# A fused RWKV-7 state update and gated convolution: chunks of 64 tokens, every product on 64x64 tiles of TensorE, decays by scans both ways

## The chip, the cores and the metric

The kernel runs on one core of a Trainium2 chip. A core has TensorE (PE, with its weight loads PEld), VectorE (DVE), ScalarE (ACT), GpSimd (POOL) and SyncE (SP, which issues the DMAs). The metric is device time in microseconds from the first to the last instruction of one execution.

## The reference

A recurrence over 768 tokens for 4 x 8 = 32 independent heads of 40 channels, then a gated short convolution between two matrix products over 320 channels. All of it is float32.

```python
for t in range(S):                                     # S = 768; state is 40 x 40 for each of 32 (b, h)
    y[:, :, t] = np.einsum('bhd,bhde->bhe', rt, state)
    Sa = np.einsum('bhde,bhe->bhd', state, at)
    state = state * wt[:, :, None, :] - np.einsum('bhd,bhe->bhde', Sa, bt) + np.einsum('bhd,bhe->bhde', vt, kt)
...
gate = 1.0 / (1.0 + np.exp(-gate_pre))                 # gate_pre: causal convolution of 5 taps over x = y
out = (gate * (x @ w_val)) @ w_out                     # 320 x 320 matrices
```

## The kernel before

The tokens are cut into 24 chunks of C = 32. Inside a chunk the recurrence is turned into matrix products: a running product of the decays w (`lam`, the scan of line 344) scales a, and its inverse (logarithm and exponential on ACT, a Newton step on DVE, lines 357 to 366) scales k and b (`atil`, `ktil`, lines 371 and 377). The products of a with k and b (`amat`, line 385) give two strictly triangular 32x32 matrices for each of the 32 units (a unit is one batch and head). One is inverted by substitution on DVE: four chunks make one group whose triangles stand side by side, and 30 steps of two operations each (`step`, lines 430 and 433: a product into `tm`, a subtraction from `x`) do all of them at once, with 32x32 block transposes around them (lines 422 and 451).

The serial part runs chunk after chunk, in two halves of 16 units (`hf`): `stage_u0` (lines 492 and 493) multiplies with v and with the state, `stage_uu` (531 and 534) applies the inverted triangle, `stage_g` (560) forms the products with r, `stage_ys` (576 and 577) yields output and new state, and `stage_st` (608) transposes the state for the next chunk. Results go from PSUM to SBUF by copies on ACT and masked products on DVE. Two chunks of outputs are then moved by DMAs from units to channels (`xe` to `xt`), convolved (738, DVE), gated (748 to 753: three functions on ACT, one DVE operation and one more function on ACT), multiplied with `w_val` (85, 93), gated (769), multiplied with `w_out` (103) and stored.

In `stage_u0` each unit has two matrix products into one PSUM region: line 492 contracts over 64 rows (two units share the 128 partitions), line 493 over 128 rows, and the two alternate. `stage_uu` has products of 64 rows and 64 or 40 columns, in which four neighbouring ones use four different 64x64 quarters of the array.

`Plan` holds every operation with an engine, a length in ns and what it waits for, and makes one order for each of PE, ACT, DVE and POOL. Each engine executes its order strictly, so an operation that waits holds up all that stand behind it. Where the plan leaves PE idle, the last loop puts in matrix products on a constant tile (`dm`, line 808), whose results nobody reads; there are 364 rows of them in the trace.

The constants' loading, the conversion of the weights from 64-bit floats on DVE (lines 50 to 57), and a second path for inputs whose decays leave a range (not taken here) stand in both versions.

Of the kernel before, what the change touches and what calls it, by code (L numbers as in the profile page):

```python
# [17 lines left out]
C = 32  # L18
P16 = 16
ER = 104  # L20
DM = 320
NW = P16 * 33
NE = P16 * C
EWF = NW + 3 * NE
NWT = 1280 + DM + 15
WB = 323
UO = 184
X0 = [(0, 0, D, 0, 0), (1, 0, D, 0, 40), (2, 0, 8, 0, 120), (2, 8, 16, 1, 120), (3, 0, D, 2, 0), (2, 16, D, 2, 40)]
X1 = [(4, 0, D, 0, 80), (5, 0, D, 1, 0), (6, 0, D, 1, 40), (7, 0, D, 1, 80)]
NCST = 128 + 32 + 64 + 64 + 32 + 128  # L30
NQ, NL = 7, 8
WLO, WHI = 0.5, 2.0
NB = 1
LAT = 180
NIT = 4
FB = 3
TS = 11000
GAP = 200
TH = 5000
WIN = 3413  # L40
RHO = {"uu": 0.9, "v": 0.9, "w": 1.4, "u0": 1.3, "am": 1.4, "g": 1.4, "kbt": 1.5, "st": 1.5}
# [54 lines left out]
def out_mms(nc, ps, gv, wo, j, n):  # L96
    T = nc.tensor
    L = n * C
    if n == 2:
        for k in range(3):  # L100
            r = slice(j * 64, j * 64 + 64) if k == 2 else slice(0, 128)
            q = 8 if k == 2 else 4 * k + 2 * j
            T.matmul(out=ps, lhsT=gv[r, q * L:q * L + 128], rhs=wo[k][r], start=(k == 0), stop=(k == 2))  # L103
# [9 lines left out]
def moe_steps(nc, mo, pp, wts, wz, xe, xt, store):  # L113
    V, A = nc.vector, nc.scalar
    L, w = C, B * C
# [25 lines left out]
    out_mms(nc, ps[:, 0:DM], gv.rearrange("p b t -> p (b t)"), wo, 0, 1)  # L141
# [6 lines left out]
class Plan:  # L148
    """Operations with an engine, a length and what they wait for, put into an order engine by engine."""
# [4 lines left out]
    def op(self, name, eng, dur, deps, fn, lat=None):  # L154
        assert name not in self.ops, name
        self.ops[name] = [eng, dur, list(deps), fn, LAT if lat is None else lat]

    def order(self):
        ops = {n: [e, d, [x for x in dp if x in self.ops], f, l] for n, (e, d, dp, f, l) in self.ops.items()}
        succ = {n: [] for n in ops}  # L160
        left = {}
        for n, o in ops.items():
            left[n] = len(o[2])
            for x in o[2]:
                succ[x].append(n)
        topo, stack, cnt = [], [n for n in ops if not left[n]], dict(left)
# [10 lines left out]
        def lag(x, y):  # L177
            return ops[x][4] if ops[x][0] != ops[y][0] else (0 if ops[x][0] in ("PE", "SP") else 127)
# [5 lines left out]
        pred = {n: o[2] for n, o in ops.items()}  # L184

        def place(seq, before, gap):
            """Each operation of seq into the first gap of its engine after what it waits for."""
            free = {e: [[0.0, 1e12]] for e in {o[0] for o in ops.values()}}
            when = {}

            def find(e, t, d):
                f = free[e]
                i = bisect.bisect_right(f, [t, 1e13]) - 1
                i = max(i, 0)
                while True:
                    u = max(f[i][0], t)
                    if u + d <= f[i][1]:
                        return u
                    i += 1

            def take(e, t, d):
                f = free[e]
                i = bisect.bisect_right(f, [t, 1e13]) - 1
                lo, hi = f[i]
                f[i:i + 1] = [x for x in ([lo, t], [t + d, hi]) if x[1] - x[0] > 1]

            for n in seq:
# [750 lines left out]
```

## Time and profile before

| | before |
|---|---|
| times of three runs, us | 712.37, 716.68 (median), 718.1 |
| span of the profiled execution, us | 712.3 (the lowest of the times is 712.37) |
| mean granted TensorE clock | 0.805 of full speed |
| PE / DVE / ACT / POOL busy, us | 647.2 / 474.2 / 384.7 / 177.8 |

A busy time is the union of the engine's instructions in the trace. A float32 matrix product of the program is two MATMUL rows in the trace, a transpose on PE is one; neighbouring matrix products overlap, so the length of one row says little, and the time of a stage is read from the stretch that it fills. The granted clock has two levels here, 0.5 and 1.0 of full speed (1.2 and 2.4 GHz).

### The profile page before, as it was taken

To read this page: it belongs to the slowest core of one execution; us is meant where nothing else is said; L and a number is where in the kernel's file an instruction comes from. 1 tells how busy PE (TensorE), PEld (TensorE's weight loads), DVE (VectorE), ACT (ScalarE), POOL (GpSimd) and SP (SyncE) were. 2 spreads that over 40 slices of the span, in tenths; PEclk is the share of its full clock that TensorE was granted. 3 is DMA by queue.
4 is the path that set the end of the run, shared out by engine and by line. 5 is a ranking of instruction groups with operands and counts; after the bars stand their busy time and mean duration, and the time that the engine had idled before them with its cause. 6 is when DMAs were issued, how large, how long until landed. Compare 5 with 4: busy or idle time off the path is not lost.

```text
span 712.3 us, 19169 instructions
## 1 busy us (share of the span) xinstructions
PE 647.2 (91%) x7701; PEld 509.5 (72%) x7701; DVE 474.2 (67%) x1151; ACT 384.7 (54%) x1167; POOL 177.8 (25%) x146
## 2 busy tenths in 40 slices
PE   1687899998999989899999999999999999999983
PEld 0566787887777768677777687777778787777772
DVE  7958956358577775956766676879656646895140
ACT  3426564446457754664754547676644663556430
POOL 7674323022332250423222032122202011100000
PEclk9957766568788876867877878999968779999996
DMA  8642322142142334233241152171302121212010
GB/s 210 152 118 63 93 53 63 40 114 69 46 107 72 83 101 102 69 87 80 63 118 50 52 129 67 60 177 43 106 28 75 37 64 56 71 55 69 20 32 12
DMA packets 26400, 55.31 MB, mean 78 GB/s; under 512 B 6564, under 2 KB 17060, under 8 KB 23812
## 3 DMA queue, kind: packets, MB, share of 16 engines
q1 hardware_dynamic: 26308, 54.05, 29.2%
q8 instruction: 62, 1.02, 0.6%
q14 instruction: 30, 0.25, 0.1%
HBM read 45.90 MB, written 3.93 MB: 70 GB/s over the span
## 4 chain that ended last, share of the span: by engine, by line
PE 65%; DVE 12%; ACT 8%; DMA 7%; SPq 3%; issue 2%; POOL 1%; DVEq 0%; ACTq 0%; POOLq 0%
PE pc L493 15%; PE pc L492 14%; PE pm L103 5%; PE pm L85 4%; DMA out<-xt 4%; PE pc L576 4%; SPq L314 3%; PE pp L408 3%; PE pp L385 3%; PE sg L608 3%; PE sg L560 3%; PE pc L577 2%; PE pc L518 2%; DVE mm L569 2%; PE pc L517 2%
## 5 line engine op out<-in xcount | busy, mean ns | idle before, releaser
L493 PE MATMUL pc<-st,qa 128*64 128x64 f32 x768 | 142.8, 274 | 0.0
L492 PE MATMUL pc<-v,akb 64*64 64x64 f32 x768 | 139.8, 268 | 1.1 <-DVE xe L601 1.1
L499 ACT COPY us<-pc 64x160 f32<-64x160 f32 x96 | 27.5, 287 | 159.1 <-PE pc L493 158.4
L492 PEld LDWEIGHTS pc<-v,akb 64*64 64x64 f32 x768 | 82.5, 150 | 34.3 <-DVE xe L601 1.3
L493 PEld LDWEIGHTS pc<-st,qa 128*64 128x64 f32 x768 | 84.1, 155 | 31.2
L569 DVE TENSOR_TENSOR mm<-sg,cst 64x128 f32<-64x128 f32 x192 | 55.4, 289 | 50.4 <-PE sg L560 45.1
L738 DVE SCALAR_TENSOR_TENSOR ag<-xt,wts,ag 128x256 f32<-128x256 f32 (+2 forms) x156 | 65.7, 449 | 16.6 <-ACT ag L736 16.4
L576 PE MATMUL pc<-mm,lh 128*40 128x80 f32 x768 | 71.9, 248 | 1.8 <-DVE mm L569 1.6
L577 PE MATMUL pc<-mm,lh 128*40 128x80 f32 x768 | 70.6, 248 | 2.5 <-DVE mm L569 2.5
L371 POOL TENSOR_TENSOR qa<-ew,lam 40x512 f32<-40x512 f32 x24 | 45.1, 1879 | 105.5 <-PE pc L493 93.3
L417 ACT COPY lh<-pp 64x160 f32<-64x160 f32 x192 | 55.1, 287 | 30.0 <-PE pp L408 26.1
L377 POOL TENSOR_TENSOR kb<-ew,y 104x512 f32<-104x512 f32 x24 | 47.9, 1997 | 79.0 <-PE pp L408 47.1
L576 PEld LDWEIGHTS pc<-mm,lh 128*40 128x40 f32 x768 | 60.5, 126 | 7.2 <-DVE mm L569 2.4
L577 PEld LDWEIGHTS pc<-mm,lh 128*40 128x40 f32 x768 | 59.6, 125 | 6.5 <-DVE mm L569 6.1
L430 DVE TENSOR_TENSOR tm<-x 128x30 f32<-128x30 f32 (+9 forms) x180 | 63.2, 351 | 1.5
L471 POOL MEMSET mm<- 40x640 f32 x22 | 13.8, 627 | 200.6 <-PE pc L576 106.5
L433 DVE TENSOR_TENSOR x<-x,tm 128x30 f32<-128x30 f32 (+9 forms) x180 | 60.8, 338 | 1.7
L617 ACT COPY lh<-sg 40x160 f32<-40x160 f32 x184 | 52.8, 287 | 15.1 <-PE sg L608 12.9
L542 ACT COPY vu<-pc 40x128 f32<-40x128 f32 x192 | 49.8, 260 | 16.0 <-PE pc L534 13.4
L551 ACT COPY mm<-pc 32x160 f32<-32x160 f32 x192 | 54.4, 284 | 2.8
L456 POOL TENSOR_TENSOR akb<-akt,cst 128x512 f32<-128x512 f32 x24 | 35.9, 1494 | 69.7 <-PE pc L492 56.5
L385 PE MATMUL pp<-kb,qa 104*64 104x64 f32 x768 | 38.4, 267 | 16.3 <-POOL kb L377 14.5
(109 smaller groups left out, 1209.4 us busy)
## 6 DMA issues: line engine op xcount, KB each, us to landing
ew<-in_ew SPq DMA_DIRECT2D x24, 838.5 KB
vu<-in_vt SPq DMA_DIRECT2D x24, 416.0 KB
mm<-in_rp SPq DMA_DIRECT2D x48, 100.0 KB
v<-in_v SPq DMA_DIRECT2D x24, 160.0 KB
mm<-in_vn SPq DMA_DIRECT2D x48, 80.0 KB
out<-xt SPq DMA_DIRECT2D x24, 160.0 KB
xt<-xe SPq DMA_DIRECT2D x66, 42.5 KB
ag<-in_wts SPq DMA_DIRECT2D x3, 323.0 KB
```

What stands on the lines that cost most here:

```text
L385: T.matmul(out=st_["ap", c][b2 * 64:b2 * 64 + 64, u * 64:u * 64 + 64], lhsT=QA[c % NQ][0:ER, p], rhs=st_["kb", c][:, p], start=True, stop= ...
L417: A.copy(out=dst[:, i], in_=pv[i * 64:i * 64 + 64, :, par * 64:par * 64 + D])
L430: V.tensor_tensor(out=tv, in0=x[:, j:j + 1, j + 1:32].to_broadcast([128, j, n]), in1=x[:, 0:j, j:j + 1].to_broadcast([128, j, n]), op=ALU. ...
L433: V.tensor_tensor(out=x[:, 0:j, j + 1:32], in0=x[:, 0:j, j + 1:32], in1=tv, op=ALU.subtract)
L492: T.matmul(out=o, lhsT=akb[r, u], rhs=v4[r, u * D:u * D + 64], start=True, stop=False)
L493: T.matmul(out=o, lhsT=qa[:, p], rhs=st[:, p - 8 * hf], start=False, stop=True)
L551: A.copy(out=dst, in_=src)
L569: V.tensor_tensor(out=dst, in0=ps[r, :, par], in1=maskG[r].unsqueeze(1).to_broadcast([64, 4, C]), op=ALU.mult)
L576: T.matmul(out=ps[0:40, hl, b * 80:b * 80 + 80], lhsT=lh[:, 0, p * D:p * D + D], rhs=mm[:, 0, :, p], start=True, stop=True)
L577: T.matmul(out=ps[64:104, hl, b * 80:b * 80 + 80], lhsT=lh[:, 1, p * D:p * D + D], rhs=mm[:, 1, :, p], start=True, stop=True)
L617: A.copy(out=dst[:, i], in_=pv[i * 64:i * 64 + 40, :, r0:r0 + D])
L738: V.scalar_tensor_tensor(out=acc[:, q], in0=xt[:, q, i:i + L], scalar=cw[:, k, i:i + 1], in1=acc[:, q], op0=ALU.mult, op1=ALU.add)
```

## The change

The kernel's fast path is written anew. The chunk is 64 tokens, so there are 12; the serial part is passed through 12 times.

**Decays.** One scan gives the running product over 64 tokens (`LAM`, line 306); a second scan, over the same data from the back and started for each unit with the reciprocal of the product's last value (line 548, 16 numbers), gives its inverse (line 308). The logarithm, the exponential and the Newton step are gone.

**Products on 64x64 tiles.** Each unit stands alone on 64 partitions and 64 columns (40 channels padded to 64, or 64 tokens). Every stage of the serial part issues products of four quarters of the array in turn. Where two products add into one PSUM region (`pairs`), the first of each pair stands in a first half of the stage and the second in the second half, with a drain of PE between.

**Triangles.** The inverse of a 64x64 triangle is made of two inverted 32x32 triangles, by the same 30 steps of two DVE operations, and a corner that two small stages on PE form from them (`fmat`, `zmat`, 32x32 tiles). A group is two chunks, which fill the same 128 x 1024 numbers as four chunks of 32 did; there are 7 groups (one chunk, five times two, one chunk). POOL clears the upper half before the steps (`tri`) and spreads the result (`expand`).

**The rest.** The masks are applied on POOL (`akm`, `gm`), to tiles that ACT has copied from PSUM, and the scaling of a, k and b is on POOL from the third chunk on. The gate is one Sigmoid. The matrix products on the constant tile are gone. The plan has other lengths and no repeated passes, and now orders SP as well; PSUM tiles (P, Q, R, M, two banks each) have one holder at a time.

```diff
-C = 32
+C, GC = 64, 32
...
-    A.activation(out=gv, in_=acc, func=AF.Abs)
-    A.activation(out=gv, in_=gv, func=AF.Exp, scale=-1.0)
-    A.activation(out=gv, in_=gv, func=AF.Ln, bias=1.0)
-    V.scalar_tensor_tensor(out=acc, in0=acc, scalar=0.0, in1=gv, op0=ALU.min, op1=ALU.subtract)
-    A.activation(out=acc, in_=acc, func=AF.Exp)
+    A.activation(out=acc, in_=acc, func=AF.Sigmoid)
...
+    def scan(c, back):
+        w = W[c % 2]
+        if not back:
+            V.memset(ind2[:, 0:NW - 1:C + 1], 1.0)
+            V.tensor_tensor_scan(out=LAM[c % NA].rearrange("p u t -> p (u t)"), data0=w[:, 0:NW - 1], data1=ind2[:, 0:NW - 1], initial=0.0, op0=ALU.mult, op1=ALU.max)
+        else:
+            V.tensor_tensor_scan(out=w[:, 1:NW][:, ::-1], data0=w[:, 1:NW][:, ::-1], data1=ind2[:, 1:NW][:, ::-1], initial=0.0, op0=ALU.mult, op1=ALU.max)
...
+    def atil(c, eng):
+        eng.tensor_tensor(out=AT[c % NA], in0=AT[c % NA], in1=LAM[c % NA][:, :, 0:C], op=ALU.mult)
+    def ktil(c, hf, eng):
...
+        eng.tensor_tensor(out=k, in0=k, in1=inv(c)[:, q].unsqueeze(2).to_broadcast([ER, 8, 2, C]), op=ALU.mult)
+    def amat(c, hf):
+        p = st_["P"] = ps("P")
+        for i in range(8):
+            u = 8 * hf + i
+            o = slice(i * C, i * C + C)
+            for e in H2:
+                a = AT[c % NA][rows[e], u]
+                for x, h in ((e, e), (1 - e, 1 - e)):
+                    T.matmul(out=p[halves[h], 0 if x == e else 1, o], lhsT=KB[0][rows[e], u, x], rhs=a, start=True, stop=True)
+    def aev_l(c, hf):
+        g, j = gof[c]
+        for q in range(4):
...
+            A.copy(out=LS[g % 2][r, :, j * 16 + 8 * hf:j * 16 + 8 * hf + 8].rearrange("p t m -> p m t"),
+                   in_=st_["P"][r, 0].rearrange("p (u t) -> p u t", t=C)[:, :, x0:x0 + 32])
+    def akm(c, hf, eng):
+        a = AK[c % NA][:, 8 * hf:8 * hf + 8]
+        eng.tensor_tensor(out=a, in0=a, in1=maskS.unsqueeze(1).to_broadcast([128, 8, C]), op=ALU.mult)
...
+    def tri(g):
+        G.affine_select(out=X, in_=X, pattern=[[1, 32], [-1, 32]], base=0, channel_multiplier=0, compare_op=ALU.is_ge, fill=0.0)
+    def step(j, half):
+        n = 31 - j
+        tv = TM[:, 0:j * n].rearrange("p (t s) -> p t s", s=j)
+        o = X[:, j + 1:32, 0:j]
+        if half == 0:
+            V.tensor_tensor(out=tv, in0=X[:, j + 1:32, j:j + 1].to_broadcast([128, n, j]), in1=X[:, j:j + 1, 0:j].to_broadcast([128, n, j]), op=ALU.mult)
+        else:
+            V.tensor_tensor(out=o, in0=o, in1=tv, op=ALU.subtract)
...
+    def pairs(off, dia):
+        for ph in H2:
+            if ph:
+                T.drain()
+            for i in range(8):
+                for f in ((off, dia) if ph == 0 else (dia, off)):
+                    for e in H2:
+                        f(e, ph if f is off else 1 - ph, i, dict(start=i == 0 and ph == 0, stop=ph == 1, skip_group_check=True))
+    def stage_u0(c):
+        p = st_["Q"] = ps("Q")
+        def off(e, b, i, kw):
+            u = 8 * b + i
...
+            T.matmul(out=p[halves[e], b, i * D:i * D + D], lhsT=AK[c % NA][halves[1 - e], u], rhs=VN[c % 2][halves[1 - e], u], **kw)
+        def dia(e, b, i, kw):
+            u = 8 * b + i
+            if c:
+                T.matmul(out=p[halves[e], b, i * D:i * D + D], lhsT=AT[c % NA][rows[e], u], rhs=ST[c % 2][rows[e], u], **kw)
+        pairs(off, dia)
...
+    def gm(c, hf, eng):
+        eng.tensor_tensor(out=GS[hf], in0=GS[hf], in1=maskS.unsqueeze(1).unsqueeze(1).to_broadcast([128, 2, 8, C]), op=ALU.mult)
...
+        op(("at", c), "DVE" if early else "POOL", 1140 if early else 2400, [("sf", c), ("lda", c)], lambda c=c, e=V if early else G: atil(c, e))
...
-    with tc.manual_schedule(engines={E.PE, E.Activation, E.DVE, E.Pool}):
-        V.memset(dm, 1.0)
...
-                k = max(int((t - pe) // GAP), min(int((t - pe) // 122), int((TH - work) // 290)))
-                for i in range(k):
-                    T.matmul(out=PCT[0][0:64, 1, 440:512], lhsT=dm[:, 0:64], rhs=dm, start=True, stop=True)
+    with tc.manual_schedule(engines={E.PE, E.Activation, E.DVE, E.Pool, E.SP}):
         for t, e, d, n, fn in seq:
             fn()
```

On PE, `stage_u0` of one half before (`v` and `akb` are of 64 rows, `st` and `qa` of 128), and the end of `stage_u0` of one chunk after, with what follows it:

```order
L492 MATMUL pc_119<-v_101,akb 64x64
L493 MATMUL pc_119<-st_103,qa_93 64x64
L492 MATMUL pc_119<-v_101,akb 64x64
L493 MATMUL pc_119<-st_103,qa_93 64x64
L492 MATMUL pc_119<-v_101,akb 64x64
```

```order
L439 MATMUL Q<-vn_102,ak_83 64x40 x2
L444 MATMUL Q<-st_107,at_72 64x40 x2
L439 MATMUL Q<-vn_102,ak_83 64x40 x2
L444 MATMUL Q<-st_107,at_72 64x40 x2
L439 MATMUL Q<-vn_102,ak_83 64x40 x2
L415 MATMUL P<-tt_99,fs_100 32x32 x32
L495 MATMUL R<-cst,st_107 40x40 x32
```

The alternation of 64 and 128 rows is gone; all products of the stage stand on quarters of the array, and the stage is followed by one on 32x32 tiles.

On DVE, steps of one group before, and the start of the steps of one group after (x is the triangles, tm the products; ag is the convolution, st and xe the state and the output of the serial part):

```order
L433 TENSOR_TENSOR x<-x,tm 128x2x29
L430 TENSOR_TENSOR tm<-x 128x84
L738 SCALAR_TENSOR_TENSOR ag<-xt,wts,ag 128x256
L585 TENSOR_TENSOR st_105<-pc_120,lam 104x8x40
L601 TENSOR_TENSOR xe<-pc_120,lam 104x8x32
L433 TENSOR_TENSOR x<-x,tm 128x3x28
L344 SCALAR_TENSOR_TENSOR lam<-ew,ind 104x528
L430 TENSOR_TENSOR tm<-x 128x108
```

```order
L368 STREAM_TRANSPOSE x_95<-ls_93 128x1024
L378 TENSOR_TENSOR tm_97<-x_95 128x30
L380 TENSOR_TENSOR x_95<-x_95,tm_97 128x30
L378 TENSOR_TENSOR tm_97<-x_95 128x58
L380 TENSOR_TENSOR x_95<-x_95,tm_97 128x29x2
L378 TENSOR_TENSOR tm_97<-x_95 128x84
L380 TENSOR_TENSOR x_95<-x_95,tm_97 128x28x3
L378 TENSOR_TENSOR tm_97<-x_95 128x108
```

Before, other operations stand between the steps; after, the 60 operations of a group stand in one piece, with one small copy between them at most, and state and output of the serial part wait in front of or behind the piece.

On POOL, a stretch before and one after (mm is cleared rows; kb, qa and at are k, b and a scaled; ak and gs are masked products; tt is the spread inverse):

```order
L471 MEMSET mm_86 40x640
L472 MEMSET mm_86 40x640
L371 TENSOR_TENSOR qa_88<-ew,lam 40x16x32
L456 TENSOR_TENSOR akb<-akt,cst 128x512
L377 TENSOR_TENSOR kb<-ew,y_2902 104x16x32
```

```order
L326 TENSOR_TENSOR kb_70<-kb_70,w_68 104x1024 x2
L321 TENSOR_TENSOR at_72<-at_72,lam_77 104x1024
L515 TENSOR_TENSOR gs_115<-gs_115,cst 128x1024
L356 TENSOR_TENSOR ak_82<-ak_82,cst 128x512
L515 TENSOR_TENSOR gs_116<-gs_116,cst 128x1024
L371 AFFINE_SELECT x_95<-x_95 128x1024
```

POOL's clearing operations give way to products with two operands, twice as long; there are 66 of 1024 columns and 24 of 512 in all, against 72 of 512 before.

## Rows read from the trace of the kernel before

**Rows 1.** The page's head: the span, then busy us, share and instructions of each engine.

```profile
span 712.3 us, 19169 instructions
PE 647.2 (91%) x7701; PEld 509.5 (72%) x7701; DVE 474.2 (67%) x1151; ACT 384.7 (54%) x1167; POOL 177.8 (25%) x146
```

**Rows 2.** Busy us by stretch: PE, PEld, DVE, ACT, POOL, granted clock, DMA share, GB/s.

```profile
0.00:50.00 50.00, 25.61 (x213) 21.02 (x213) 39.54 (x73) 16.95 (x41) 37.21 (x37) 0.89 0.67 170
50.00:650.00 600.00, 573.58 (x6899) 450.44 (x6898) 414.27 (x1008) 344.16 (x1052) 140.55 (x109) 0.79 0.29 76
650.00:713.00 63.00, 48.04 (x593) 38.01 (x591) 20.39 (x71) 23.64 (x75) 0.00 (x0) 0.85 0.10 23
```

**Rows 3.** The page's chain of waits that ended last, by engine.

```profile
PE 65%; DVE 12%; ACT 8%; DMA 7%; SPq 3%; issue 2%; POOL 1%; DVEq 0%; ACTq 0%; POOLq 0%
```

**Rows 4.** Stretches as in 2, matrix products into pc alone: stage_u0 at either clock.

```profile
201.20:205.60 4.40, 4.18 (x32) 1.00 0.74 190
112.20:118.80 6.60, 6.60 (x38) 0.50 0.00 0
```

**Rows 5.** The same with the inverse, ttb: one stage_uu, then two of them.

```profile
261.80:262.90 1.10, 0.69 (x32) 1.00 0.08 29
285.50:287.60 2.10, 1.99 (x64) 0.50 0.27 78
```

**Rows 6.** The same for pm: line 103 with six rows, then line 85 with twelve.

```profile
482.30:484.60 2.30, 2.00 (x6) 1.00 0.26 71
530.10:534.00 3.90, 3.74 (x6) 0.50 0.01 2
...
470.00:471.70 1.70, 1.60 (x12) 1.00 0.83 182
578.20:581.30 3.10, 2.93 (x12) 0.50 0.31 92
```

**Rows 7.** Groups on DVE: columns and number | busy us, mean ns | idle before, releaser.

```profile
L430 DVE TENSOR_TENSOR tm<-x 128x30 f32<-128x30 f32 (+9 forms) x180 | 63.2, 351 | 1.5
L433 DVE TENSOR_TENSOR x<-x,tm 128x30 f32<-128x30 f32 (+9 forms) x180 | 60.8, 338 | 1.7
```

**Rows 8.** The same on DVE, shapes apart.

```profile
L344 DVE TENSOR_TENSOR_SCAN lam<-ew,ind 104x528 f32<-104x528 f32 x24 | 33.2, 1384 | 3.4 <-DMA ew<-in_ew 3.4
L738 DVE SCALAR_TENSOR_TENSOR ag<-xt,wts,ag 128x256 f32<-128x256 f32 x88 | 45.0, 523 | 6.9 <-ACT ag L736 6.8
L738 DVE SCALAR_TENSOR_TENSOR ag<-xt,wts,ag 128x128 f32<-128x128 f32 x60 | 21.3, 361 | 9.7 <-ACT ag L736 9.6
L422 DVE STREAM_TRANSPOSE x<-lst 128x1024 f32<-128x1024 f32 x7 | 8.6, 1234 | 0.7 <-ACT lst L397 0.7
L451 DVE STREAM_TRANSPOSE tt<-x 128x1024 f32<-128x1024 f32 x7 | 13.7, 1953 | 0.1
L585 DVE TENSOR_TENSOR st<-pc,lam 104x320 f32<-104x320 f32 x46 | 22.4, 487 | 17.3 <-PE pc L577 16.5 <-ACT wz L711 0.3
L601 DVE TENSOR_TENSOR xe<-pc,lam 104x256 f32<-104x256 f32 x48 | 20.0, 416 | 0.1
```

**Rows 9.** DVE in order of time: start, length, operation.

```profile
121.51 1.37 DVE L430 TENSOR_TENSOR tm<-x 128x234 f32<-128x234 f32 x1
122.91 1.26 DVE L433 TENSOR_TENSOR x<-x,tm 128x234 f32<-128x234 f32 x1
124.20 0.41 DVE L430 TENSOR_TENSOR tm<-x 128x238 f32<-128x238 f32 x1
```

**Rows 10.** POOL in order of time: the same stretch, then an undisturbed one.

```profile
120.52 2.09 POOL L377 TENSOR_TENSOR kb<-ew,y 104x512 f32<-104x512 f32 x1 [1.01 <-PE pp L408]
122.69 1.22 POOL L371 TENSOR_TENSOR qa<-ew,lam 40x512 f32<-40x512 f32 x1
...
334.18 1.27 POOL L456 TENSOR_TENSOR akb<-akt,cst 128x512 f32<-128x512 f32 x1
```

**Rows 11.** ACT, shapes apart: a copy whose output is strided.

```profile
L397 ACT COPY lst<-pp 128x256 f32<-128x256 f32 x24 | 14.5, 604 | 9.8 <-PE pp L385 4.8 <-DVE akt L402 4.8
```

More of the change, by code (lines that the diff above doesn't have):

```diff
@@ new lines, in greedy @@
+                for q in succ[n]:
+                    cnt[q] -= 1
+                    if not cnt[q]:
+                        ready[ops[q][0]][q] = max(when[x] + ops[x][1] + lag(x, q) for x in pred[q])
+            return when
+        when = greedy({n: -level[n] for n in ops})
+        self.span = max(when[n] + ops[n][1] for n in ops)
+        return [(when[n], ops[n][0], ops[n][1], n, ops[n][3]) for n in sorted(ops, key=lambda n: (when[n], idx[n]))]
+DMAS = {"ldw", "lda", "ldk", "ldv", "ldt", "ldr", "cst", "wd", "xd", "store"}
@@ new lines, in fmat, with fev @@
+    def fmat(c):
+        p = st_["P"] = ps("P")
+        g, j = gof[c]
+        for u in range(P16):
+            for h in H2:
+                r, b = slice(h * 64, h * 64 + 32), slice(h * 64 + 32, h * 64 + 64)
+                T.matmul(out=p[b, 0, u * 32:u * 32 + 32], lhsT=ML[c % 2][r, u], rhs=TN[r, :, j * 16 + u], start=True, stop=True)
+    def fev(c):
+        for h in H2:
+            b = slice(h * 64 + 32, h * 64 + 64)
+            A.copy(out=FS[b], in_=st_["P"][b, 0].rearrange("p (u t) -> p u t", t=32))
@@ new lines, in u0e, with stage_u @@
+    def u0e(c):
+        A.copy(out=U0[:, 0:P16 * D].rearrange("p (b x) -> p b x", b=2), in_=st_["Q"][:, :, 0:8 * D])
+    def stage_u(c, hf):
+        p = st_["Q"] = ps("Q")
+        for i in range(8):
+            u = 8 * hf + i
+            for e in H2:
+                t = TT[c % 2][halves[e], u].rearrange("p x t -> p (x t)")
+                T.matmul(out=p[halves[e], 0, i * D:i * D + D], lhsT=t, rhs=U0[halves[e], u * D:u * D + D], start=True, stop=True)
+                T.matmul(out=p[halves[1 - e], 1, i * C:i * C + C], lhsT=U0[halves[e], u * D:u * D + C], rhs=t, start=True, stop=True)
@@ new lines, in stage_g, with ge @@
+    def stage_g(c, hf):
+        p = st_["R"] = ps("R")
+        for i in range(8):
+            u = 8 * hf + i
+            for e in H2:
+                f = 1 - e
+                r_ = RT[c % 2][rows[f], u]
+                T.matmul(out=p[halves[f], 0, i * C:i * C + C], lhsT=VT[0][rows[f], u], rhs=r_, start=True, stop=True)
+                T.matmul(out=p[halves[e], 1, i * C:i * C + C], lhsT=UT[hf][rows[f], i], rhs=r_, start=True, stop=True)
+    def ge(c, hf):
+        A.copy(out=GS[hf].rearrange("p x u t -> p x (u t)"), in_=st_["R"])
@@ L689, in fast_path @@
-        if gof[c][2] == 0:
-            pairs = [c0 for c0, n in groups if c0 < c]
-            op(("xe", c), "DVE", 90, (both("evac_y", c - 1) if c else []) + (both("xd", pairs[-2]) if len(pairs) > 1 else both("w", 0) + both("w", 1) if pairs else []), lambda c=c: new_xe(c))
+            op(("kt",) + k, "DVE" if early else "POOL", 1140 if early else 2400, [("sb", c), ("ldk", c)], lambda c=c, hf=hf, e=V if early else G: ktil(c, hf, e))
+            op(("am",) + k, "PE", 980, [("kt",) + k, ("at", c), ("gd1", c), ("begin", g - 2), ("end", g - 2)] + [("exp", x) for x in (groups[g - 2] if g > 1 else [])] + [("fm", c - 2), "lsz"] + [("u0", q)], lambda c=c, hf=hf: amat(c, hf),
+               slot="P", readers=[("aev_l",) + k, ("aev_m",) + k, ("aev_a",) + k])
@@ new lines, in fast_path @@
+            op(("kbe",) + k, "ACT", 590, [("kbt",) + k], lambda c=c, hf=hf: kbe(c, hf))
+        if j == len(groups[g]) - 1:
+            op(("begin", g), "DVE", 1240, [("aev_l", x, h) for x in groups[g] for h in H2] + [("end", g - 1), ("endn", g - 1)], lambda g=g: begin(g))
+            op(("tri", g), "POOL", 1150, [("begin", g)], lambda g=g: tri(g))
+            prev = ("tri", g)
+            for s in range(1, 31):
+                for half in H2:
+                    nm = ("step", g, s, half)
+                    op(nm, "DVE", (70 if OV else 170) + s * (31 - s) * 1.04, [prev], lambda s=s, half=half: step(s, half))
+                    prev = nm
+            op(("diag", g), "DVE", 60, [prev], lambda: diag())
+            op(("end", g), "DVE", 1240, [("diag", g)], lambda g=g: end(g, 0))
+            op(("endn", g), "DVE", 1970, [("diag", g)] + [("fm", x) for x in (groups[g - 1] if g else [])], lambda g=g: end(g, 1))
@@ L796, in fast_path, with val @@
-    A.preload_act_table_set("natural_log_exp_and_others")
+                op(("cv", c, i, k), "DVE" if i else "ACT", 65 + 1.17 * n if i else 60 + .85 * n, [("cv", c, i - 1, k)] if i else both("xd", c) + wl + [("gv", c - 1)],
+                   lambda i=i, k=k, cv=cv: cv(i, k))
+        op(("gate", c), "ACT", 600, [("cv", c, 4, k) for k in range(3)], lambda: A.activation(out=acc, in_=acc, func=AF.Sigmoid))
+        def val(xt=xt):
+            p = st_["M"] = ps("M")
+            for m in range(3):
+                val_mms(nc, p[:, m // 2, m % 2 * 256:m % 2 * 256 + (256 if m < 2 else 128)], wv, xt, m, C)
```

874 lines of the change are left out of this document (309 added, 565 removed).

## The prediction

> **What bounds the kernel now.** I read the page's head first, then the busy times by stretch, then the chain of waits, then single stages. PE is busy 647 us of a span of 712.3 [rows 1], in the middle 573.6 of 600 [rows 2], and holds 65% of the chain that ended last [rows 3]; no other engine is near: DVE has 414 of these 600 us. So PE's stages bound the kernel, at a granted clock of 0.79 there.
>
> Within PE one stage stands out. `stage_u0` of one half, 16 products of 64 columns, fills 4.18 us at the full clock and 6.60 at half of it (the latter stretch has 38 rows, 6 of the next stage) [rows 4]. `stage_uu`, also 16 products of at most 64 columns, fills 0.69, and two of them at half clock 1.99 [rows 5]. The difference is the order: the first alternates contractions over 64 and 128 rows, the second turns through four quarters of the array. Of `stage_u0` there are 48: 48 x 4.18 = 201 us even at full clock, more than a quarter of the span.
>
> **What PE costs afterwards.** Per chunk of 64: `amat` 64 products, `stage_u0` 64, `stage_u` 64, `stage_g` 64, `stage_s` 64, `stage_y` 96, all on quarters. That is 416, or 13 times 32. By [rows 5] 32 such products take 0.69 + (0.69 - 0.2 of tail) = 1.2 us, at half clock 2.0: 15 us, or 26. `val` and `out` work on the same sizes per 64 tokens as before: twelve rows of line 85 take 1.60 us (2.93), twice, half as much again for the narrow third, and two times six rows of line 103 at 2.00 (3.74) [rows 6]: 4.0 + 4.0 = 8 us (15). The transposes and the two small stages are 128 products with two tiles at a time, at most twice the price of four: an estimate of 5 us (10). The sum is 28 us per chunk at full clock, 51 at half. At the clock of now, 0.8, it is 28 / 0.8 = 35 us, times 12 is 420 us. PE falls from first to second place.
>
> **DVE becomes the bound.** Its work, operation by operation:
>
> The 30 steps: 124.0 us for the six full groups of before [rows 7], 20.7 each, now 7 groups: 145 us. The saving of the first group, which ran 14 shorter steps, is given up. Transposes: two of 1.23 and one of 1.95 per group [rows 8]: 31 us. Scans: two per chunk over 1040 numbers, 1.38 x 1040 / 528 = 2.73 us each [rows 8], 24 of them: 65 us. Convolution: unchanged per 64 tokens, 8 x 0.523 + 4 x 0.361 = 5.6 us [rows 8], 12 times: 67 us. State: three operations of 640 columns; from 256 to 320 columns 0.416 goes to 0.487 [rows 8], 1.1 ns a column, so 0.84 us each, 32 of them: 27 us. Output: 0.416 + 768 x 0.0011 = 1.26 us, 12 times: 15 us. The gating product: 0.70 + 0.27 us, 12 times: 12 us. The scalings of the first two chunks: six of 1.26 us: 8 us. The conversion of the weights, clears, reciprocals and the halo: 29 us, an estimate from the 39.5 us that DVE works in its first 50 [rows 2], most of which stays. The sum is 399 us, against 474 now. The gate's one DVE operation and three ACT functions go; ACT, at 385 us of 712, is no bound, and its new strided copies of 0.60 us [rows 11], eight per chunk, take it nowhere near one.
>
> **What POOL takes from DVE.** POOL has 66 products of 1024 and 24 of 512 columns: 156 halves at the undisturbed 1.27 us [rows 10] are 198 us, with seven selections of 1 to 2.5 us about 210. Before it had 72 x 1.27 = 91. In [rows 9, 10] two operations of the step chain that take 0.41 us undisturbed took 1.37 and 1.26 while POOL had two products under way. The chain lost 1.8 us to 2 x 1.27 of POOL, 70%. A DVE operation with two operands in SBUF and a POOL product evidently go one after the other. What the DVE rows above already hold of this belongs to POOL's 91 us; the other 120 us cost DVE between nothing (all in its idle time) and 120. I take half, 60 us, since about four fifths of DVE's work is of the kind that is hit, but not all its span is work. The Trainium skill (SBUF — State Buffer, "Who interferes with whom") gives the pair as an exclusive lock, held for a whole instruction; [rows 9, 10] agree with it, and by it the term would stand nearer to its upper end.
>
> **Idle time of DVE.** At the start: it idles 10.5 us in its first 50 now [rows 2], and the new first group needs two loads, two scans, products and strided copies before a step can begin: 20 us (10 to 30). At the end: it idles 42.6 of the last 63 us [rows 2], and the tail (spread, corner, u, g, y, moves, convolution, two products, store) is as long: 40 us. In the middle DVE idles 186 of 600 us while PE binds [rows 2]. Now DVE leads, but PE with 420 us is not far behind, the serial part waits out each piece of 60 steps, and DVE's order has ten places per two chunks where it waits for another engine (transposes, selection, state, output, first taps, gating). Between 0 and 186 I take half: 93 us.
>
> **The sum.** 399 + 60 + 20 + 40 + 93 = 612 us, to be held against the span of 712.3, beside which the profiled execution's own time (the lowest of the three, 712.37) has next to nothing. The median of the runs is 4.3 us above that; I add as much: **616 us**. The bounds of the terms, POOL's 0 to 120 and half to one and a half times the middle idle time, give 555 to 700.
>
> **Rivals.**
> *POOL falls into idle time.* The serial part leaves DVE waits long enough for POOL's 120 us: 399 + 20 + 40 + 93 = 552, with the 4 us 556. For it: in [rows 10] the products are short and come in bursts. Against: the steps stand in one piece, and POOL's operations become ready just then. 15%.
> *The lock in full.* All 120 us fall on DVE: 676 us. This is the page's rule where DVE never leaves the pair unclaimed; a chain of dependent steps, which lets POOL in between any two [rows 9], is such a place, but the middle idle time isn't. 10%.
> *Two row halves in one PSUM bank take turns.* Before, each half of the rows wrote its own bank (`ps[r, b2, ...]`); now, in `amat`, `stage_u`, `stage_g` and all of `pairs`, both halves write one bank, on different partitions. If they take turns, the 13 x 32 products cost 2 x 1.2 us: PE 40 us per chunk, 50 at a clock of 0.8, 600 in all, and it binds again: 600 + 60 for start and end + some 30 = 690. The Trainium skill (TensorEngine Tiling (Array Packing), "Gotcha 1: PSUM Pressure") says that different row tiles cannot access one PSUM bank at the same time; no row of before shows the case. 7%.
> *The clock falls, and the kernel is slower than before.* The products on the constant tile go, and PE works 28 us out of some 50 per chunk. The middle was granted only 0.79 although PE was 96% busy there [rows 2]. If it stays at half clock nearly throughout, PE needs 51 x 12 = 612 us, start and end add 60 in which it does little, and the waits of the middle, since DVE's 459 us and PE's 612 stand in one serial chain, another 70: about 742 us. It decides from a mean granted clock of about 0.55 on. Against it: a stage on four quarters has the array far fuller than `stage_u0`, and in [rows 4, 5] the stretches that were granted the full clock are of both kinds. 10%.
> *It doesn't do what it says*, as strided or reversed operands cost double on POOL, DVE or PE, and nothing is left: within 1%. 3%.
>
> **How the numbers follow.** The forecast has 55%, with its own range of 575 to 660. The predicted time is that case's. For 8 in 10 I leave out the falling clock (10%), the case of no change (3%) and half of the first rival, and reach from 555 to 705. Below 709 lie the forecast, the first three rivals (all but a part of the third): 86% faster by over 1%; 4% within 1%, which is about what a measurement can tell; 10% slower.
>
> **What would show it.** `stage_u0` over a whole chunk in under 2.5 us at full clock; stages of 32 products near 1.2 us. DVE as the busiest engine in the middle, over 400 us, with steps of 0.4 us that take over 2 when POOL is at work. A mean granted clock between 0.65 and 0.85. The last 60 us with DVE mostly idle. It is wrong if PE is over 85% busy (bank or clock), if POOL's products take far more than 2.5 us undisturbed, or if DVE idles over a third of the middle.

## The result, and the profile after

The changed kernel takes 650.09 us (median of four runs, 648.69 to 651.48) against 717.39 for the kernel before: a ratio of 0.905, with a 95% interval of 0.9005 to 0.910. The forecast was 616 us. It is faster by 67 us, where 101 were forecast. The times below are medians of each kernel's runs; a run that was more than 1.5% longer than the fastest of the same kernel, at a lower granted clock, is left out of them.

The head of the page after, to be held against [rows 1]:

```profile
span 648.1 us, 28086 instructions
PE 418.7 (65%) x12929; PEld 371.1 (57%) x12929; DVE 461.9 (71%) x782; ACT 250.7 (39%) x458; POOL 225.1 (35%) x111
```

PE fell from 647 to 419 us and DVE is now the busiest engine. But no engine is near the span, and the chain that ended last, which was 65% PE [rows 3], is divided evenly between PE and DVE:

```profile
PE 35%; DVE 34%; issue 11%; DMA 8%; ACT 4%; SPq 4%; POOL 3%; DVEq 0%; ACTq 0%; POOLq 0%
```

The busy times by stretch, in the columns of [rows 2] (PE, PEld, DVE, ACT, POOL, granted clock, DMA share, GB/s):

```profile
0.00:50.00 50.00, 9.84 (x224) 9.02 (x224) 26.08 (x48) 15.42 (x30) 13.63 (x18) 1.00 0.66 164
50.00:600.00 550.00, 389.84 (x12380) 347.57 (x12382) 427.87 (x715) 229.84 (x420) 209.17 (x92) 0.75 0.25 67
600.00:649.00 49.00, 18.98 (x329) 14.54 (x325) 7.97 (x20) 5.48 (x9) 2.35 (x1) 0.73 0.09 28
```

DVE idles 24 us at the start, 41 at the end and 122 of the 550 in between. The longest waits over the whole run, by what DVE waited for (total us, times, longest us); 78 of their 92 us lie in the middle:

```profile
DVE xe L534 <- PE R L526: 30.4, 5, 7.8
DVE ag L660 <- PE M L86: 22.1, 4, 11.5
DVE x L368 <- ACT ls L343: 19.9, 6, 7.9
DVE st L484 <- PE Q L470: 19.7, 4, 8.3
```

They are few and long: three of the four are for one large stage of PE, the third for ACT's strided copies of the triangles. The 60 operations of a group stand in one piece, with one small copy in between at most, in four of the seven groups only; between those of the first, the sixth and the last stand one to six larger operations (scalings, a scan, state, output, gating).

**TensorE.** The products into Q in two short stretches (length, busy, rows, granted clock), which are `stage_u0` over a whole chunk, once at each clock:

```profile
281.75:284.85 3.10, 2.58 (x128) 1.00 0.74 180
150.55:154.65 4.10, 3.88 (x128) 0.50 0.80 191
```

And those of line 336, `amat` of one half with 32 products:

```profile
263.65:264.95 1.30, 1.16 (x64) 1.00 0.12 25
316.95:319.05 2.10, 1.99 (x64) 0.50 0.04 8
```

64 products of `stage_u0` fill 3.0 us from first to last, with the drain in the middle, where 16 filled 4.18 [rows 4]. The passes of `amat` that stand wholly at full clock fill 1.16 to 1.35 us.

**VectorE.** The groups that answer to [rows 7, 8]: the two lines of a step, the convolution and the scans (back, then forward).

```profile
L378 DVE TENSOR_TENSOR tm<-x 128x30 f32<-128x30 f32 (+14 forms) x210 | 94.5, 450 | 13.1 <-POOL x L371 6.2
L380 DVE TENSOR_TENSOR x<-x,tm 128x30 f32<-128x30 f32 (+14 forms) x210 | 86.3, 411 | 6.9
L644 DVE SCALAR_TENSOR_TENSOR ag<-xt,wts,ag 128x256 f32<-128x256 f32 (+1 forms) x144 | 78.3, 605 | 25.5 <-ACT ag L642 16.3
L308 DVE TENSOR_TENSOR_SCAN w<-w,ir 104x1040 f32<-104x1040 f32 x12 | 45.0, 3750 | 0.3
L306 DVE TENSOR_TENSOR_SCAN lam<-w,ir 104x1040 f32<-104x1040 f32 x12 | 32.3, 2696 | 4.2 <-DMA w<-in_w 3.8
```

A step took 351 and 338 ns on average before, and takes 450 and 411. One backward scan shows why, in the order of time (start, length), first on DVE, then on POOL:

```profile
310.59 13.30 DVE L308 TENSOR_TENSOR_SCAN w<-w,ir 104x1040 f32<-104x1040 f32 x1
```

```profile
310.34 2.19 POOL L321 TENSOR_TENSOR at<-at,lam 104x1024 f32<-104x1024 f32 x1
312.48 2.88 POOL L394 TENSOR_TENSOR tt<-ls,cst 128x1024 f32<-128x1024 f32 x1
315.29 2.38 POOL L515 TENSOR_TENSOR gs<-gs,cst 128x1024 f32<-128x1024 f32 x1
317.58 2.90 POOL L394 TENSOR_TENSOR tt<-ls,cst 128x1024 f32<-128x1024 f32 x1
320.40 1.31 POOL L356 TENSOR_TENSOR ak<-ak,cst 128x512 f32<-128x512 f32 x1
```

The scan, 2.3 us long where POOL is quiet, stood through a whole row of POOL's products, which followed each other without a gap, and ended 2.2 us after the last of them.

### The profile page after: what moved, and what is told of

The parts are those of the page before. It is cut to its first block, busy times and chain, and to the rows that moved or that the text cites. A ratio compares the mean times of both kernels' runs of the same rounds, so it can differ in the third digit from the quotient of the medians.

```text
span 648.1 us, 28086 instructions
## 1 busy us (share of the span) xinstructions
PE 418.7 (65%) x12929; PEld 371.1 (57%) x12929; DVE 461.9 (71%) x782; ACT 250.7 (39%) x458; POOL 225.1 (35%) x111
## 4 chain that ended last, share of the span: by engine, by line
PE 35%; DVE 34%; issue 11%; DMA 8%; ACT 4%; SPq 4%; POOL 3%; DVEq 0%; ACTq 0%; POOLq 0%
DVE tm L378 12%; DVE x L380 11%; PE M L96 5%; SPq L289 4%; PE P L336 3%; PE M L78 3%; DMA out<-os 3%; DMA kb<-in_kb 2%; PE P L403 2%; ACT ls L343 2%; PE Q L444 2%; DMA ag<-in_wts 2%; PE P L415 2%; PE R L530 2%; PE R L524 2%
## 5 line engine op out<-in xcount | busy, mean ns | idle before, releaser
L378 DVE TENSOR_TENSOR tm<-x 128x30 f32<-128x30 f32 (+14 forms) x210 | 94.5, 450 | 13.1 <-POOL x L371 6.2
L515 POOL TENSOR_TENSOR gs<-gs,cst 128x1024 f32<-128x1024 f32 x24 | 57.7, 2407 | 129.5 <-ACT gs L512 129.5
L644 DVE SCALAR_TENSOR_TENSOR ag<-xt,wts,ag 128x256 f32<-128x256 f32 (+1 forms) x144 | 78.3, 605 | 25.5 <-ACT ag L642 16.3
L380 DVE TENSOR_TENSOR x<-x,tm 128x30 f32<-128x30 f32 (+14 forms) x210 | 86.3, 411 | 6.9
L343 ACT COPY ls<-P 32x256 f32<-32x256 f32 x96 | 56.7, 591 | 67.3 <-PE P L336 62.9
L326 POOL TENSOR_TENSOR kb<-kb,w 104x1024 f32<-104x1024 f32 x20 | 45.7, 2308 | 73.7 <-DMA kb<-in_kb 64.3
L394 POOL TENSOR_TENSOR tt<-ls,cst 128x1024 f32<-128x1024 f32 x12 | 40.5, 3387 | 58.2 <-DVE ls L387 53.3
L530 PE MATMUL R<-gs,kt 64*64 64x64 f32 x768 | 50.1, 253 | 7.4 <-issue 5.9
L526 PE MATMUL R<-gs,kt 64*64 64x64 f32 x768 | 51.7, 232 | 1.3 <-issue 1.3
L524 PE MATMUL R<-rt,sd 40*64 40x64 f32 x704 | 49.3, 234 | 1.3 <-issue 1.3
L526 PEld LDWEIGHTS R<-gs,kt 64*64 64x64 f32 x768 | 47.6, 147 | 2.1 <-issue 2.0
L96 PE MATMUL M<-wts,ag 128*128 128x320 f32 (+1 forms) x144 | 47.6, 535 | 1.2 <-DVE ag L661 1.2
```

What stands on the lines that cost most here:

```text
L96: T.matmul(out=ps[:, j, 0:DM], lhsT=gv[r, q * L:q * L + 128], rhs=wo[k][r], start=(k == 0), stop=(k == 2))
L326: eng.tensor_tensor(out=k, in0=k, in1=inv(c)[:, q].unsqueeze(2).to_broadcast([ER, 8, 2, C]), op=ALU.mult)
L343: A.copy(out=LS[g % 2][r, :, j * 16 + 8 * hf:j * 16 + 8 * hf + 8].rearrange("p t m -> p m t"), in_=st_["P"][r, 0].rearrange("p (u t) -> p ...
L378: V.tensor_tensor(out=tv, in0=X[:, j + 1:32, j:j + 1].to_broadcast([128, n, j]), in1=X[:, j:j + 1, 0:j].to_broadcast([128, n, j]), op=ALU. ...
L380: V.tensor_tensor(out=o, in0=o, in1=tv, op=ALU.subtract)
L515: eng.tensor_tensor(out=GS[hf], in0=GS[hf], in1=maskS.unsqueeze(1).unsqueeze(1).to_broadcast([128, 2, 8, C]), op=ALU.mult)
```

## The experiments

Two questions: which part of the change is the gain, and what holds the changed kernel at 650. All ratios are against the kernel before; the changed kernel's is 0.905.

### One loop of the old kernel in another order

```diff
-        for q in range(4):
-            for b2 in range(2):
-                T.matmul(out=o, lhsT=akb[r, u], rhs=v4[...64 wide], start=True, stop=False)
-                T.matmul(out=o, lhsT=qa[:, p], rhs=st[...64 wide], start=False, stop=True)
+        for k in range(2):
+            if k: T.drain()
+            for q in range(4):
+                for b2 in range(2):
+                    if k == 0: T.matmul(out=o, lhsT=akb[r, u], rhs=v4[...40 wide], start=q == 0, ...)
+                    else: T.matmul(out=o, lhsT=qa[:, p], rhs=st[...40 wide], start=False, stop=True, ...)
```

> The kernel before, with one loop of stage_u0 regrouped: all 8 products over 64 rows of a half first, a drain, then all 8 over 128 rows, each 40 columns wide; nothing else. Theory A (the alternating order of row heights was what bound the kernel before): a stage falls from 4.18 us to about 1.4 at full clock, 48 stages, so 133 us of PE's 647 at full clock, more at half; time 560 to 630 us, as much as the whole change brought or more. Theory B (16 products that contract over up to 128 rows cost this in any order, and the gain of the change came from having half as many serial passes): the stage stays over 3.5 us and the time over 690.

Measured: 601.32 us, ratio 0.839 (0.833 to 0.845). Theory A, and more than the whole change brought. The page's busy times:

```profile
PE 478.2 (79%) x7701; PEld 388.7 (65%) x7701; DVE 489.2 (81%) x1151; ACT 385.7 (64%) x1167; POOL 181.3 (30%) x146
```

One stage, as the products into pc of a stretch:

```profile
255.95:257.45 1.50, 1.33 (x32) 1.00 0.86 226
```

The stage fills 1.42 us from first to last instead of 4.18, and PE lost 169 us. That could still be the 40 columns, so they were tried alone:

```diff
-                o = ps[r, b2, q * D:q * D + 64]        # and 64 columns of v4 and st
+                o = ps[r, b2, q * D:q * D + D]         # and 40 columns of v4 and st, order as before
```

> The kernel before with stage_u0's 16 products at 40 columns instead of 64, in the old alternating order: the part of the regrouped kernel that is not the order. Theory A (the order is the price): a stage stays near 4.18 us at full clock and the time between 695 and 725 us. Theory B (the wider, overlapping products are the price, and the regrouping gained by its 40 columns): the stage falls below 2.5 us and the time below 640.

Measured: 711.25 us, ratio 1.0008 (0.995 to 1.007). One stage:

```profile
237.30:241.30 4.00, 3.86 (x32) 1.00 0.19 53
```

The order is the price: 3.86 us in turn, 1.42 in two groups. 15 changes of the row height became one, so a change costs (3.86 - 1.42) / 14 = 0.17 us at full clock, if nothing else in the order has a price.

### The alternation put back into the changed kernel

```diff
-        pairs(off, dia)          # off, off, dia, dia: all on 64 rows
+        mixed(off, dia)          # off, dia, off, dia
-            lhsT=AK[c % NA][halves[1 - e], u], rhs=VN[c % 2][halves[1 - e], u]
+            lhsT=AK[c % NA][:, u], rhs=VN[c % 2][:, u]
```

> The changed kernel with the alternation put back into stage_u0: the products with v contract over 128 rows (over both row halves, so that the sum holds a second unit's part) and stand in turn with those of 40 rows with the state; the number of products is the same. Theory A: 64 products go from 3.0 us (4.0 at half clock) to 4 x 4.18 = 16.7 us, 12 times 13.7 or more is 164 us of PE in the serial part; PE binds again, time 750 to 860 us. Theory B: the products over 128 rows take two quarters in place of one, the stage at most doubles to 6 us, 12 x 3 = 36 us more, time 650 to 690.

Measured: 826.54 us, ratio 1.156 (1.146 to 1.166). Theory A again. A stage (products into Q) at half clock, where the changed kernel took 4.0:

```profile
194.20:217.80 23.60, 23.39 (x128) 0.50 0.07 19
```

All eleven full stages ended at half clock. In the old order the two products of a pair also follow each other into one PSUM region; here neighbouring products write different banks and the price is there all the same, so it isn't that. With the runs before it makes the case from both sides: the order of row heights decides over 115 us in the old kernel and, with the taller products that it takes, 176 in the new.

### What POOL takes from DVE

```diff
-        eng.tensor_tensor(out=GS[hf], in0=GS[hf], in1=mask, op=ALU.mult)
+        eng.tensor_tensor(out=one element, ...); eng.memset(GS[hf], 0.0) x2; eng.memset(half of GS[hf], 0.0)
# and so for akm, atil, ktil and expand
```

> The changed kernel with every product on POOL (masks, scalings, spread) replaced by a product of one element and clears of the same tile that last about as long (2.5 clears of 0.95 us for 1024 columns, 3 for the spread); the values are gone, the order, the lengths and the waits stay. Theory A (POOL's products keep DVE from its second operand, and DVE binds): no DVE step is held up any more, DVE's busy time falls from 462 to about 400 us and the time by nearly as much, to 585 to 610. Theory B (what POOL costs DVE lies in time that DVE would wait anyway, and the serial hand-offs between PE, ACT and POOL bind): DVE's busy time falls as well, but the time stays over 630.

Measured: 605.63 us, ratio 0.852 (0.843 to 0.861): theory A's time. The page's busy times:

```profile
PE 416.3 (69%) x12929; PEld 369.7 (62%) x12929; DVE 358.1 (60%) x782; ACT 250.6 (42%) x458; POOL 253.7 (42%) x381
```

The two lines of a step, the convolution and the scans (groups on DVE), and the middle of the run (busy us by stretch):

```profile
L395 DVE TENSOR_TENSOR tm<-x 128x30 f32<-128x30 f32 (+14 forms) x210 | 69.6, 332 | 16.5 <-POOL x L388 9.5
L397 DVE TENSOR_TENSOR x<-x,tm 128x30 f32<-128x30 f32 (+14 forms) x210 | 69.6, 332 | 6.9
L667 DVE SCALAR_TENSOR_TENSOR ag<-xt,wts,ag 128x256 f32<-128x256 f32 (+1 forms) x144 | 53.4, 433 | 27.2 <-ACT ag L665 18.0 <-DMA xt<-xe 9.0
L306 DVE TENSOR_TENSOR_SCAN lam<-w,ir 104x1040 f32<-104x1040 f32 x12 | 27.9, 2325 | 3.5 <-DMA w<-in_w 3.1
```

```profile
50.00:550.00 500.00, 385.83 (x12364) 344.49 (x12365) 323.27 (x708) 230.13 (x420) 236.45 (x350) 0.77 0.27 73
```

Clears on POOL, though they take longer in all, hold no step up. DVE's own work is therefore 358 us, and POOL's products add 104 to it, half of their own 209 us. But of these 104 only 44 are time (48 by the spans of the profiled executions): DVE idles 177 of 500 us in the middle now, 55 more than before.

### Masks and the spread off POOL

```diff
-  op(("ge",) + k, "ACT", 910, ...ge);  op(("gm",) + k, "POOL", 2400, ...gm on GS)
+  op(("gm",) + k, "DVE", 1230, [("g",) + k, ("cst",)], ...gm from PSUM)
```

> The changed kernel with one mask moved: gm, 24 products of 1024 columns on POOL behind a copy on ACT, becomes one product on DVE that reads PSUM. POOL loses 58 us, ACT 24 x 0.91 = 22, DVE gains 24 x 1.22 = 29 and loses a quarter of POOL's interference, some 16 to 25; the way from stage_g to stage_y loses 0.91 + 2.4 - 1.2 = 2.1 us, 24 times. Theory A (hand-offs in the serial part cost as much as DVE's work): time 610 to 640. Theory B (DVE's own sum binds alone, 29 more and 16 to 25 less): 645 to 665.

Measured: 637.69 us, ratio 0.890 (0.883 to 0.898), theory A: 12 us faster than the change. DVE's sum fell from 462 to 446 us although it took over 29, but it waits 36 us for `stage_g` now.

```diff
-  eng.tensor_tensor(out=TT[c % 2], in0=LS...broadcast, in1=maskP...)          # POOL
+  for q in range(4): A.copy(out=TT[c % 2][r, :, q % 2], in_=LS[g % 2][r, ...])  # TT cleared once
```

> The changed kernel with gm on DVE from PSUM (637.7 us) and, on top, the spread (expand) moved from POOL to four copies on ACT per chunk: POOL loses another 37 us, ACT gains 48 copies of 0.6 to 0.96 us, 29 to 46. POOL's interference with DVE shrinks by about the same share, 10 to 20 us of DVE's time. Theory A (DVE's held-up steps set the time): 615 to 630 us. Theory B (waits on PE's results set it): 633 to 642.

Measured: 628.84 us, ratio 0.880 (0.869 to 0.890). That is the upper end of theory A, but the interval overlaps that of the run above, so the run hardly parts the two theories. DVE's busy time fell by another 23 us, to 423, and the time by about 9.

### The steps left out

```diff
     def step(j, half):
+        return
```

> The changed kernel without the 420 operations of the steps (the triangles are not inverted; the plan keeps their places, so that every other operation stands where it stood). That takes 181 us of DVE's busy time away, 139 of it its own by the length of a step that nothing holds up (0.332 us), the rest POOL's. Theory A (DVE's time is the kernel's time): 470 to 520 us. Theory B (PE and the hand-offs stand right behind DVE, as the 104 us less on DVE that gave only some 45 us of time say): 540 to 600 us, PE the busiest engine by far.

Measured: 581.2 us (one run of two). Theory B. The page's busy times and its chain, then DVE's longest waits:

```profile
PE 411.0 (71%) x12929; PEld 364.9 (63%) x12929; DVE 284.6 (49%) x362; ACT 250.6 (43%) x458; POOL 224.3 (39%) x111
...
PE 63%; DMA 12%; ACT 10%; issue 9%; SPq 3%; DVE 2%; POOL 1%; ACTq 0%; POOLq 0%; DVEq 0%
```

```profile
DVE st L485 <- PE Q L471: 73.4, 9, 18.1
DVE xe L535 <- PE R L527: 42.9, 10, 7.8
```

With 177 us less work on DVE the kernel is 69 us faster. PE's stages, what passes between them and the rest of DVE's work stand at some 580 us already: with all of DVE's steps to do the kernel is only an eighth longer.

### The clock and the plan

Is it PE's clock, a mean of 0.769? Products on the constant tile went back into PE's planned gaps.

```diff
+                    for i in range(int((t - pe) // 200)):     # 297 products; dense: // 122, 986 products
+                        T.matmul(out=st_["Q"][0:64, 0, 440:512], lhsT=dm[:, 0:64], rhs=dm, ...)
```

> The changed kernel with products on a constant tile put back into PE's planned gaps, one of 64 rows by 72 columns per 200 ns of gap, 297 in all. Theory A (at a mean granted clock of 0.769 PE's stages cost up to 1.7 times their full-clock length, and PE holds 35% of the chain): the clock rises to 0.85 or more and the time falls to 615 to 640 us. Theory B (the gaps are waits on DVE, which PE's speed does not shorten, or the products stand in the way of stages that come ready): the time stays within 1% of 650 or rises.

> The changed kernel with 986 products on the constant tile in PE's planned gaps, one per 122 ns of gap, where the run with 297 raised the mean granted clock only from 0.769 to 0.807 and the time did not change. Theory A (the clock is what PE's 63% of the chain without the steps comes from, and 297 were too few): the clock reaches 0.88 or more and the time falls to 610 to 640 us. Theory B (what a faster clock gives back, the products take, since they stand ahead of stages that come ready late): the clock rises, the time stays within 1.5% of 650 or rises.

Measured: 653.19 us at a clock of 0.807, ratio 0.913 (0.901 to 0.925), and 670.06 us at 0.860, ratio 0.939 (0.933 to 0.944). Theory B both times: the denser set is slower by more than its interval. Its products keep PE busy for long:

```profile
L687 PE MATMUL Q<-dm 128*64 128x72 f32 x1972 | 151.5, 242 | 13.7 <-ACT us L461 7.4 <-DVE st L483 3.3 <-DVE st L485 2.3
```

What a higher clock alone would be worth can't be read from this, since the products that raise it also stand in the way. But the runs of the changed kernel differ in their mean clock by themselves: 649.76 us at 0.769, 648.69 at 0.830, 650.42 at 0.777 and 651.48 at 0.775. So a mean clock higher by 0.06 came with 1 us less, and the 0.807 of the 297 products lies within what the kernel has without them.

Or is it an order made for lengths that don't hold?

```diff
-  aev_l 1060, akm 1250, am/u/g 980, u0 2100, fm/zm 880, s 1500, st 1160, y 3600, val 3400, out 2800, step 170 +
+  aev_l 2400, akm 1500, am/u/g 1500, u0 3500, fm 2000, zm 1500, s 2400, st 1900, y 5000, val 4500, out 4200, step 205 +
```

> The changed kernel with nothing but the plan's lengths changed to nearer those of its trace: the strided copies of one half from 1060 to 2400 ns, the akb mask from 1250 to 1500, a step from 170 to 205 ns plus its columns, and PE's stages from lengths at the full clock to ones between the two clocks (amat, u, g 980 to 1500, u0 2100 to 3500, f 880 to 2000, z 880 to 1500, s 1500 to 2400, st 1160 to 1900, y 3600 to 5000, val 3400 to 4500, out 2800 to 4200). The order of every engine changes with them. Theory A (DVE's 122 us of idle time in the middle come from an order made for lengths that do not hold): 615 to 638 us. Theory B (the waits lie in the structure, and an order for other lengths only moves them): within 1.5% of 650 us, or longer.

Measured: 658.4 us, ratio 0.922 (0.914 to 0.930). Theory B: an order for lengths nearer to the measured ones is no better.

### The old kernel with the change's cheap parts

```diff
# on top of the regrouped stage_u0, still in chunks of 32
-  Ln, Exp (ACT) and two Newton operations (DVE) for 1 / lam
+  V.reciprocal(out=ind[:, 33:NW:33], in_=lam[:, :, C]); a second scan from the back, in place in w
-  Abs, Exp, Ln (ACT), one operation on DVE, Exp (ACT)
+  A.activation(out=a_, in_=a_, func=AF.Sigmoid)
```

> The kernel before with stage_u0 regrouped (601 us) and, on top, the change's decays by scans both ways and its Sigmoid gate, still in chunks of 32. ACT loses 24 x (0.63 + 0.63) = 30 us of logarithm and exponential and 15 x 3 x 0.63 = 28 us of gate functions; DVE loses 24 x (0.86 + 0.81) = 40 us of Newton step and 10.2 us in the gate, and gains 24 x (1.38 + 0.24 + 0.07) = 41 us of second scans, reciprocals and clears. Theory A (DVE, 81% busy, is next in line, and its sum hardly changes): 585 to 600 us. Theory B (the hand-offs between ACT and DVE that go with them are what the serial part waits for): below 580. Theory C (the second scan, which must wait for the guards on ACT, starts late and pushes the products back): over 605.

Measured: 578.74 us, ratio 0.806 (0.798 to 0.814), the fastest of all: 71 us below the changed kernel. The time is B's by 1 us; which of the two mechanisms it was, this run can't say, since DVE's work and ACT's hand-offs went together. Its busy times:

```profile
PE 459.4 (80%) x7787; PEld 375.8 (65%) x7787; DVE 469.6 (81%) x1160; ACT 332.4 (58%) x1074; POOL 155.4 (27%) x146
```

DVE's sum fell from 489.2 to 469.6, 20 us where 9 were worked out, and the span by 24. The operations exchanged come to those 9 (50.0 us of Newton and gate against 40.5 of scans, reciprocals and clears); most of the rest, 8 us, is convolution and scalings that were held up less. Here, then, the time fell by about as much as DVE's work, which speaks for A's mechanism without showing it.

```diff
-                for i in range(k):
-                    T.matmul(out=PCT[0][0:64, 1, 440:512], lhsT=dm[:, 0:64], rhs=dm, start=True, stop=True)
```

> The regrouped kernel before with scans both ways and the Sigmoid gate (579 us), now without the 182 products on the constant tile, 364 rows. Theory A (they keep the clock at 0.883, and PE, 80% busy, needs it): the clock falls below 0.85 and the time rises to 585 to 605 us. Theory B (with stage_u0 regrouped PE no longer binds, and the products only fill idle time): within 1% of 579.

Measured: 581.62 us, ratio 0.812 (0.805 to 0.819), clock 0.889. Theory B: the products on the constant tile are worth nothing once `stage_u0` is regrouped, and the clock did not need them.

## Why the prediction was right, and where it was off

**TensorE's part was right.** `stage_u0` was named as the stage that bounds the kernel and its order as the reason, and the two orders on both kernels show it. PE's sum was put at 420 us and is 419, in part by luck: at the measured clock of 0.769 the forecast's 28 us per chunk would come to 437. 32 products on quarters were put at 1.2 us, or 2.0 at half clock, and fill 1.16 and 1.99. Only `stage_u0` itself misses its mark, 3.0 us against "under 2.5": PE idles 0.3 us at its drain, and the products alone take more than the mark.

**DVE's sum was right by luck, its parts were not.** 399 + 60 = 459 stands against 462. By the run with clears it is 358 + 104: the first term was 41 us too high, the second, half of a bound, 44 too low, and the two nearly cancel. Some 30 of the 41 lie in three places: a step is 332 ns and not 345, a scan 2.3 us and not 2.73, the convolution 53 us and not 67. In part the lengths of [rows 7, 8], taken as DVE's own, held POOL's interference already; in part they were added where they overlap (144 operations of the convolution at 433 ns are 62 us, and fill 53).

**The term that failed is the idle time in the middle:** 93 us forecast, 122 measured. Start (20 against 24) and end (40 against 41) held. These are the 34 us that the forecast was short by: 3 on DVE's sum, 4, 1 and 29 are 37, less 1 by which the last window reaches beyond the span, less 2 since the median lies 2.0 above the span and not 4.3. Behind the size stands a wrong picture. The prediction made DVE the bound, with PE in second place, and took half of the old idle time. But 104 us less work on DVE gave 44 us, and 177 less gave 69: PE's stages, at half clock for about half of the middle, and the hand-offs around them stand at 580 us even without the steps. In the changed kernel neither engine binds alone; they take turns.

**The rivals.** *POOL falls into idle time* was right in part: of DVE's 104 us, some 60 do. *The lock in full* was wrong as a time, right in how one operation suffers (13.3 us for a scan of 2.3). The Trainium skill (SBUF — State Buffer, "Who interferes with whom") gives the pair as an exclusive lock for a whole instruction, between a DVE operation with two inputs in SBUF and a POOL operation that reads SBUF, not one that only writes it; the steps of 332 ns beside clears, and of 450 and 411 beside products, agree. The scan goes further: it waited through four products that POOL began after it, and not through one instruction. *Row halves in one bank take turns* is out: in `amat` both row halves write one bank, and 32 products fill 1.16 us at full clock. That different row tiles cannot access one PSUM bank at the same time, as the Trainium skill says (TensorEngine Tiling (Array Packing), "Gotcha 1: PSUM Pressure"), does not show in this layout. *The clock falls* did not come: 0.769, inside the 0.65 to 0.85 of the forecast.

**Two sums that do not add up.** The bounds of the two terms, both low or both high, come to 510 and 723 us, not to 555 and 700. And doubling the 15 us of products on quarters makes 43 us per chunk, not 40, so the rival of the banks stood at some 735 us, over the old time.

**What the prediction did not ask.** It priced the change, not its parts. The regrouped loop alone is worth 115 us, scans and Sigmoid some 23 more. Chunks of 64 on quarters, with all that comes with them (the masks on POOL, the corner, the new plan), therefore cost 71 us against the old structure with the same order, scans and gate. Moving one mask and the spread off POOL takes 21 of them back. The other 50 are DVE's waiting: in that kernel it has 47 us less work than in the best one, 423 against 470, and idles 96 us more, 204 of 627 against 108 of 578. Other plan lengths and filler products did not take the waiting away, and without the steps DVE idles 295 of 579. The old kernel passes its serial part in two halves of 16 units, which can fill each other's waits; the changed one has one `stage_u0`, state update and output for all 32. That this is the reason is argued only, as is the part that the longer stages themselves have in it; halves in the changed kernel were not tried.

## What to carry to other kernels

Where one stage stands out, price the smallest edit to that stage beside the whole rewrite: here a reordered loop gave more than the rewrite that contained it. A duration read while another engine interferes holds that interference; take it from an undisturbed row, and put the interference in one place. When the busiest engine has 70% of the span, what is taken off it is worth the part that the next engine's waits don't swallow, about two fifths here (44 of 104 us, 69 of 177).

## What the runs showed of the hardware

A change between products of 64 and of 128 rows cost 0.17 us at full clock. At half clock, in the changed kernel with the alternation put back (128 and 40 rows), a stage took 23.5 us against 4.0, with 62 more changes: 0.31 us each, what the taller products cost by themselves included.

Of DVE and POOL, the engine that had its next operation ready went on, and the other waited. POOL's products in a row kept a scan waiting for 11 us, as shown above. DVE did the same to POOL: the end of a scan and ten operations of the convolution, each begun 0.08 us before the end of the one before it, stretched one product of 512 columns, 1.27 us undisturbed, to 5.50:

```profile
231.57 5.50 POOL L356 TENSOR_TENSOR ak<-ak,cst 128x512 f32<-128x512 f32 x1 [1.22 <-ACT ak L352]
```

```profile
229.16 3.38 DVE L308 TENSOR_TENSOR_SCAN w<-w,ir 104x1040 f32<-104x1040 f32 x1
232.46 3.48 DVE L644 SCALAR_TENSOR_TENSOR ag<-xt,wts,ag 128x256 f32<-128x256 f32 x10
235.87 1.25 DVE L538 COPY xe<-xe 104x64 f32<-104x64 f32 x1
```

The copy behind them has one operand, in SBUF, and was held up too: its median over the run is 0.20 us, and here it took 1.25, to the end of POOL's product. DVE operations with one operand in PSUM (line 484, 0.81 us) kept their length beside POOL's products: the longest of the twenty took 0.83.

The two small stages of 32 products on 32x32 tiles differ: at full clock line 415 fills 1.20 us and line 403 the 1.98 below; at half clock they fill 1.92 and 2.01, so line 403 gained next to nothing from the faster clock. In it the moving operand has its columns 128 bytes apart; that this is the reason was not tested.

```profile
249.15:251.25 2.10, 1.98 (x64) 1.00 0.38 93
```
